# A grouped-query decode kernel: six instructions fewer on GpSimd, credits given elsewhere, and one 16-slot piece at the end of the last V tile

## The chip, the cores and the metric

One core of a Trainium2 chip. The metric is the device time of one execution in microseconds (us), as the median over runs. The profile's span (first to last instruction of the program) is about 1.85 us shorter than that time. Engines are named PE (TensorE), DVE (VectorE), ACT (ScalarE), POOL (GpSimd) and SP (SyncE). One run of the kernel before, at 670.34 us with a granted clock of 0.554 (0.80 to 0.82 in its other runs), was slow and is left out everywhere.

## The reference

Decode attention for 32 query heads in 8 groups, one query each, 65,536 keys, head width 128, bfloat16:

```python
B, Hq, Hkv, Sq, Sk, D = 1, 32, 8, 1, 65536, 128
k = jnp.repeat(k, rep, axis=1); v = jnp.repeat(v, rep, axis=1)
scores = jnp.einsum("bhqd,bhkd->bhqk", q, k) * D ** -0.5
return jnp.einsum("bhqk,bhkd->bhqd", softmax(scores), v)
```

K and V are 268 MB together and each byte is read once (the page: 268.44 MB read from HBM).

## The kernel before

K and V stream through three 8 MB buffers (`io`). A tile is half a group's K or V: 128 partitions with 256 slots of 128 values each. SP issues all loads. DVE transposes K, PE scores it, ACT takes the exponential, and PE multiplies with V. PE and DVE run loops. SP, ACT and POOL run straight through their programs. Semaphores are taken (waited for and subtracted), so a loop pass that has no load of its own for a piece finds credits there that some engine gave earlier.

The last V tile comes in pieces, so that PE can follow the landings closely:

```python
TAIL = 32
CUTS = [0, 128, 192, 224, 232, 240, 248, 252, 256]
...
pe.matmul(out=pl, lhsT=sel[:, :], rhs=vs[:, ...], start=True, stop=True).then_inc(s_pt, 1)
for t in range(SL - TAIL, SL):            # the last 32 slots: "the four-column products"
    if t in CUTS:
        pe.wait_ge(s_v[CUTS.index(t)], 16)
    if t == CUTS[-2]:
        pe.wait_ge(s_dv, d_last)          # DVE's sum of what the wide products made
        gather(D, start=False, stop=False)
    i = pe.matmul(out=fin, lhsT=et[:, 1, w0:w0 + H], rhs=io[:, t, :], ...)
i.then_inc(s_pe, 1)
```

POOL clears four buffers, makes an identity, gives initial credits, and then fills the score weights `wz` once per group (eight times 4 copies):

```python
GP.mark(gp.memset(wz[:, :, :], 0.0))
GP.mark(gp.memset(vs[:, :], 0.0))
GP.mark(gp.memset(ex[:, :, :], 0.0))
GP.mark(gp.memset(vy[:, :, :], 0.0))
n = GP.mark(gp.memset(ident[:, :], 0.0))
... identity ...
gp.sem_inc(s_vd, 2)
gp.sem_inc(s_cl, 1)
for s in (s_k[1, 64], s_k[1, 192]):
    gp.sem_inc(s, 16 * (G - 1))
gp.sem_inc(s_v[1], 16 * (2 * G - 3))
gp.sem_inc(s_v[2], 16)
...
for g in range(G):
    ...  GP.wait((s_sc, 16 * g)); gp.sem_inc(s_sd, 1); at g == 1 four more credits
    for a in range(4): gp.tensor_copy(wz ...)
```

Of the kernel before, what the change touches and what calls it, by code (L numbers as in the profile page):

```python
# [15 lines left out]
P = 128  # L16
D = 128
SL = 256
KEYS = P * SL
G = 8  # L20
# [1 line left out]
WB = 160  # L22
PS = 64
TAIL = 32
CUTS = [0, 128, 192, 224, 232, 240, 248, 252, 256]


class Queue:
# [21 lines left out]
def kernel(  # L50
# [9 lines left out]
    fp32 = mybir.dt.float32  # L60
    bf16 = mybir.dt.bfloat16
# [4 lines left out]
    def sb(name, shape, dt):  # L66
        return ctx.enter_context(nc.sbuf_tensor(name, shape, dt))
# [4 lines left out]
    def sem(name):  # L72
        return ctx.enter_context(nc.semaphore(name))
# [12 lines left out]
    nrow = sb("nrow", [1, 32, H], fp32)  # L86
    nmb = sb("nmb", [P, 1], fp32)
    rl = sb("rl", [H, 1], fp32)
    ex = sb("ex", [P, 4, 512], bf16)
    et = sb("et", [P, 2, 512], bf16)  # L90
    vs = sb("vs", [P, D + 2], fp32)
    vy = sb("vy", [P, D, 4], fp32)
    vz = vy[:, :, :].rearrange("p d y -> p (d y)").rearrange("p (y d) -> p y d", d=D)
    fall = sb("fall", [H, G - 1, D + 2], fp32)
    r7 = sb("r7", [H, G - 1], fp32)
# [9 lines left out]
    s_q, s_st = sem("s_q"), sem("s_st")  # L105
    s_v = [sem(f"s_v{i}") for i in range(len(CUTS) - 1)]
    s_dv, s_ac, s_gp = sem("s_dv"), sem("s_ac"), sem("s_gp")
# [3 lines left out]
    s_sc, s_pe, s_vb, s_vc = sem("s_sc"), sem("s_pe"), sem("s_vb"), sem("s_vc")  # L111

    s_sd, s_vd, s_pt, s_ex, s_ds = sem("s_sd"), sem("s_vd"), sem("s_pt"), sem("s_ex"), sem("s_ds")
    s_cl, s_ga = sem("s_cl"), sem("s_ga")

    def down(eng, which, s, n, wait=False):

        w = dict(sync_type="semaphore", id=s.num, ant_name=s.name)
        eng.add_instruction(mybir.InstEventSemaphore(  # L119
            name=nc.get_next_instruction_name(), engine=which, sync_info=mybir.SyncInfo(  # L120
                on_wait=[mybir.SyncWait(wait_mode="sem-ge-imm", wait_value=n, **w)] if wait else [],
                on_update=[mybir.SyncUpdate(update_mode="sem-sub-imm", update_value=n, **w)],
            ),
        ))

    sp, act, dve, gp, pe = nc.sync, nc.scalar, nc.vector, nc.gpsimd, nc.tensor
# [3 lines left out]
    GP = Queue(nc, gp, s_gp)  # L130
# [5 lines left out]
    def load(src, g, b, at, s, lo=0, hi=SL):  # L136
        sp.dma_start(  # L137
            out=io[:, at * SL + lo:at * SL + hi, :], in_=rows(src, g, b)[:, lo:hi, :]
        ).then_inc(s, 16)


    k_lo = [0, 64, 128, 192]
    s_k = {(b, lo): sem(f"s_k{b}_{lo}") for b in range(2) for lo in k_lo}

    def load_k(g, b):
        SP.wait((s_sc, 16 * g - 8 + 8 * b if g else 0))
        cuts = k_lo + [SL] if (g, b) in ((0, 0), (G - 1, 1)) else [0, 128, SL] if g == 0 else [0, SL]
        for lo, hi in zip(cuts, cuts[1:]):
            load(k, g, b, 1 + b, s_k[b, lo], lo, hi)

    def values_done(n):
        SP.wait((s_vc, n))
        if n:
            sp.sem_inc(s_vd, 1)  # L154

    def load_v(g, b):
        done = 2 * (2 * g + b)
        if (g, b) == (G - 1, 1):
            SP.wait((s_vc, done - 1))
            load(v, g, b, 0, s_v[0], CUTS[0], CUTS[1])  # L160
            values_done(done)
            down(sp, mybir.EngineType.SP, s_v[2], 16)
            for lo, hi, s in list(zip(CUTS, CUTS[1:], s_v))[1:]:
                load(v, g, b, 0, s, lo, hi)
        elif (g, b) in ((G - 2, 1), (G - 1, 0)):
            SP.wait((s_vc, done - 1))
            load(v, g, b, 0, s_v[0], 0, 128)
            values_done(done)
            load(v, g, b, 0, s_v[1], 128, SL)
        else:  # L170
            values_done(done)
            load(v, g, b, 0, s_v[0])

    load_k(0, 0)
    load_k(0, 1)
    for g in range(1, G):
        for b in range(2):
            load_k(g, b)
            load_v(g - 1, b)
# [4 lines left out]
    act.dma_start(out=q_in[:, :], in_=q[0, :, 0, :]).then_inc(s_q, 16)  # L184

    GP.mark(gp.memset(wz[:, :, :], 0.0))
    GP.mark(gp.memset(vs[:, :], 0.0))
    GP.mark(gp.memset(ex[:, :, :], 0.0))
    GP.mark(gp.memset(vy[:, :, :], 0.0))
    n = GP.mark(gp.memset(ident[:, :], 0.0))  # L190
    GP.after(n)
    p_ident = GP.mark(gp.affine_select(
# [1 line left out]
        pattern=[[-1, P]], channel_multiplier=1,  # L194
    ))

    gp.sem_inc(s_vd, 2)
    gp.sem_inc(s_cl, 1)

    for s in (s_k[1, 64], s_k[1, 192]):  # L200
        gp.sem_inc(s, 16 * (G - 1))
    gp.sem_inc(s_v[1], 16 * (2 * G - 3))

    gp.sem_inc(s_v[2], 16)
# [6 lines left out]
    n = DV.mark(dve.tensor_reduce(  # L211
        out=selq[:, :], in_=ident[:, :].rearrange("p (x r) -> p r x", r=16), axis=AX.X, op=ALU.add
    ))
# [12 lines left out]
    def d_sum(g):  # L226
        return d_qT + 4 * g + 1
# [13 lines left out]
    def take(eng, which, s, n=1):  # L241
        down(eng, which, s, n, wait=True)
# [109 lines left out]
    for t in range(SL - TAIL, SL):  # L352
# [3 lines that stand above are left out]
            pe.wait_ge(s_dv, d_last)  # L356
# [103 lines left out]
    for i in range(2):  # L460
        n = DV.mark(dve.reciprocal(out=r7[:, i::2], in_=fall[:, i::2, D + i]))
    DV.after(n)
    n = DV.mark(dve.tensor_tensor(
        out=o7, in0=fall[:, :, 0:D], in1=r7[:, :, None].to_broadcast([H, G - 1, D]),
        op=ALU.mult,
    ))
# [5 lines left out]
    n = DV.mark(dve.tensor_tensor(  # L472
        out=vz, in0=vacc, in1=sely[:, :, None].to_broadcast([P, 4, D]), op=ALU.mult
    ))
    DV.after(n)
    n = DV.mark(dve.tensor_tensor(
        out=vz[:, 0:2, :], in0=vz[:, 0:2, :], in1=vz[:, 2:4, :], op=ALU.add
    ))
    DV.after(n)
    n = DV.mark(dve.tensor_tensor(  # L480
        out=vs[:, 0:D], in0=vz[:, 0, :], in1=vz[:, 1, :], op=ALU.add
    ))
# [4 lines left out]
    n = ACTQ.mark(act.activation(out=o[:, :], in_=fin, func=ACT.Copy, scale=rl[:, :]))  # L487
# [5 lines left out]
    for g in range(G):  # L493
        if g == 0:
            GP.wait((s_dv, d_qT))
            GP.after(p_ident)
        else:
            GP.wait((s_sc, 16 * g))
            gp.sem_inc(s_sd, 1)
            if g == 1:  # L500

                for t in k_lo[1:]:
                    gp.sem_inc(s_k[0, t], 16 * (G - 1))
                gp.sem_inc(s_k[1, 128], 16 * (G - 2))
        for a in range(4):
            r = slice(32 * a, 32 * a + 32)
            c0 = 28 + 32 * a
            if a == 3 and g == 1:

                take(gp, POOL, s_et)  # L510
            if a == 3:

                GP.wait((s_dv, d_sum(g)))
            gp.tensor_copy(  # L514
                out=wz[r, :, c0:c0 + H].rearrange("p (s w) h -> p s w h", s=2),
                in_=qTb[r, :, :, g, :],
            ).then_inc(s_w, 1)
# [34 lines left out]
```

## Time and profile before

| | before |
|---|---|
| median of the first three runs | 630.37 us (629.66 to 630.48) |
| span of the profiled run | 627.7 us |
| data stream, first to last packet | 1.99 to 623.77 us |
| PE, DVE busy | 57%, 55% |

The page first: the busy share of the 16 DMA engines (in tenths) and their rate in 40 slices of the span, then the DMA queues with packets, MB and share of the engines' time.

```profile
DMA  8999999999999999999999999999999999999996
GB/s 362 441 468 401 468 401 468 401 468 401 468 401 464 405 459 409 447 422 447 422 438 430 426 443 409 459 405 464 401 468 401 468 401 468 396 437 434 434 432 274
...
q1 hardware_dynamic: 6944, 268.45, 99.2%
...
q14 instruction: 2, 0.02, 0.0%
```

The kernel is bound by its DMA stream: every slice but the first and last is 90% busy or more, nearly all of it queue q1, SP's loads. What is not about the stream itself can only matter before its start, after its end, or by taking a DMA engine's time from it. The last of these shows in the DMA view of 0 to 620 us:

```profile
q1 hardware_dynamic: 6163, 267.28, 99.9%
...
q14 instruction: 1, 0.01, 0.0%
```

The last line is one instruction packet of 8 KB (0.01 MB) in the middle of the stream. The packet records of the trace place it at 518.16 us, lasting 309 ns. The trace has 16 landing records for each load, one for each of the 16 DMA engines, and the load's semaphore is waited for at 16, so these records tell how far the slowest engine is behind the others:

```
kernel before, landings of one load on 16 engines (us): second-last, last, difference
load landing before the packet    506.86   506.90   0.04
next load                         526.25   526.54   0.29
...
last piece of the last V tile     623.85   624.11   0.26
```

One engine falls behind and does not catch up (0.26 to 0.29 us in all loads from there on, but for one of 0.22), because no engine is idle from the stream's start to 620 us (q1 alone is 99.9% of the 16 engines' time). A load counts as landed only when its slowest engine is done: PE's wide products of the tail start at 621.48, behind the last landing of their piece at 621.43; the second-last was at 621.14.

The packets of the engine that falls behind can be followed by their times, as each starts within 5 ns of the end of the one before it.

```
kernel before, packets of that engine (us): start, end, ns, bytes
515.740  518.166  2426  65,536   load
518.163  518.472   309   8,192   instructions
518.469  521.238  2769  65,536   load (all other 64 KB packets of the run: 2418 to 2524 ns)
```

The instruction packet takes 0.31 us, and the load packet behind it 0.35 us more than the usual 2.42: 0.65 us in all. The engine had been 0.32 us ahead of the slowest (whose packet ended at 518.49), so it is only 0.33 us behind now. The difference of the last two landings is thus a lower bound for what a fetch takes from its engine.

The chain of waits that ended last is the tail (start, duration, what):

```profile
609.01 12.42 DMA io<-in_v_dram
...
621.48 1.03 PE acc L254 x6
...
622.53 1.80 PE pf L359 x28
624.33 0.23 PE pf L248 x2
624.56 0.24 PE pf L359 x4
...
624.89 0.36 ACT o L487
```

A DMA landing releases PE's wide products at 621.48, then come 28 four-column products, the gather over `vs` (two matmuls), the last four products, and ACT's output.

### The profile page before, as it was taken

What the parts mean: (1) busy time and instruction counts of PE and PEld (TensorE: products, weight loads), DVE (VectorE), ACT (ScalarE), POOL (GpSimd) and SP (SyncE); (2) the same over time, 40 slices, a digit from 0 to 9 for tenths busy, and PEclk for the clock granted to TensorE, in tenths of its full rate; (3) what the DMA queues carried; (4) which work ended last, traced back from release to release, by engine and by line L of the source; (5) the groups of instructions that cost most, each with busy time, mean ns of one, the idle gap of its engine ahead of it and who ended that gap; (6) DMA issues with size and microseconds to landing.
All of it is one profiled execution on the core that took longest, in us unless ns stands there. A gap on an engine that the chain in (4) does not pass through costs nothing. (4 is left out here: it accounts for less than half of the span.)

```text
span 627.7 us, 7067 instructions
## 1 busy us (share of the span) xinstructions
PE 356.4 (57%) x2142; PEld 139.8 (22%) x2142; DVE 345.5 (55%) x154; ACT 34.4 (5%) x26; POOL 9.7 (2%) x42
## 2 busy tenths in 40 slices
PE   1865483827638275381844808458193571886346
PEld 0322131312213032130321303123031230332112
DVE  7795835649066490764807557084670946684210
ACT  0000100020000200002000020000200002000100
POOL 2000000000000000000000000000000000000000
PEclk9978595967959678596785958859587695899676
DMA  8999999999999999999999999999999999999996
GB/s 362 441 468 401 468 401 468 401 468 401 468 401 464 405 459 409 447 422 447 422 438 430 426 443 409 459 405 464 401 468 401 468 401 468 396 437 434 434 432 274
DMA packets 7003, 268.49 MB, mean 428 GB/s; under 512 B 856, under 2 KB 1112, under 8 KB 1496
## 3 DMA queue, kind: packets, MB, share of 16 engines
q1 hardware_dynamic: 6944, 268.45, 99.2%
q8 instruction: 1, 0.02, 0.0%
q14 instruction: 2, 0.02, 0.0%
q10 hardware_dynamic: 56, 0.01, 0.0%
HBM read 268.44 MB, written 0.01 MB: 428 GB/s over the span
## 5 line engine op out<-in xcount | busy, mean ns | idle before, releaser
L301 PE MATMUL acc<-io,wz 128*128 x1024 | 272.7, 420 | 184.8 <-PEq L119 157.3
L373 DVE STREAM_TRANSPOSE io<-io 128x4096 uint32<-128x4096 uint32 x64 | 279.9, 4416 | 157.2 <-DVEq L119 157.2
L301 PEld LDWEIGHTS acc<-io,wz 128*128 x1024 | 106.4, 104 | 351.2 <-issue 272.5
L254 PE MATMUL acc<-io,et 128*16 128x512 bf16 x1016 | 72.5, 416 | 19.3 <-PEq L119 19.2
L440 ACT ACTIVATE ex<-acc,nmb 128x2048 bf16<-128x2048 f32 x8 | 15.7, 1967 | 556.9 <-DVE nmb L420 556.9
L410 DVE TENSOR_REDUCE mg<-acc 128x1 f32<-128x2048 f32 x8 | 18.3, 2291 | 48.3 <-DVEq L119 48.3
L254 PEld LDWEIGHTS acc<-io,et 128*16 128x16 bf16 x1016 | 27.7, 94 | 58.4 <-issue 35.5
L248 PE MATMUL pf<-vs,sel 128*4 128x130 f32 (+1 forms) x20 | 5.7, 386 | 54.2 <-PEq L119 54.2
L376 DVE STREAM_TRANSPOSE et<-ex 128x1024 bf16<-128x1024 bf16 x17 | 20.8, 1225 | 22.6 <-SPq L154 12.8
L450 ACT ACTIVATE acc<-wz 128x2560 f32<-128x2560 bf16 (+2 forms) x8 | 16.3, 2040 | 1.0 <-ACT ex L440 0.2
L412 DVE TENSOR_REDUCE m<-pt 1x4 f32<-1x128 f32 x8 | 2.2, 279 | 22.7 <-DVEq L119 22.7
L514 POOL COPY wz<-qT 32x16 bf16<-32x16 bf16 x32 | 6.1, 189 | 512.6 <-PE acc L301 440.3
L248 PEld LDWEIGHTS pf<-vs,sel 128*4 128x4 f32 x20 | 1.2, 83 | 54.7 <-issue 54.6
L326 PE MATMUL pt<-et 128*16 128x512 bf16 x32 | 13.1, 411 | 0.0
L384 DVE TENSOR_REDUCE vs<-vy 128x128 f32<-128x512 f32 x9 | 6.1, 681 | 7.6 <-DVEq L119 7.6
L423 DVE TENSOR_TENSOR vy<-acc,sely 128x512 f32<-128x512 f32 x8 | 8.5, 1064 | 0.0
L472 DVE TENSOR_TENSOR vy<-acc,sely 128x512 f32<-128x512 f32 x1 | 0.7, 691 | 11.5 <-PE acc L254 11.5
L343 PE MATMUL pb<-ident,nrow 1*128 1x1 f32 x8 | 1.6, 194 | 7.5 <-PEq L119 7.5
L326 PEld LDWEIGHTS pt<-et 128*16 128x16 bf16 x32 | 3.1, 97 | 4.5 <-issue 1.4
L341 PE MATMUL pt<-ident,mg 128*1 128x128 f32 x8 | 2.3, 283 | 2.6 <-PEq L119 2.6
L420 DVE COPY nmb<-pb 128x1 f32<-128x1 f32 x8 | 1.3, 157 | 3.9 <-DVEq L119 3.9
L343 PEld LDWEIGHTS pb<-ident,nrow 1*128 1x128 f32 x8 | 1.1, 139 | 8.9 <-issue 8.9
(31 smaller groups left out, 22.8 us busy)
## 6 DMA issues: line engine op xcount, KB each, us to landing
io<-in_v_dram SPq DMA_DIRECT2D x5, 4096.0 KB, 16.9
io<-in_k_dram SPq DMA_DIRECT2D x8, 2048.0 KB, 27.4
io<-in_k_dram SPq DMA_DIRECT2D x2, 4096.0 KB, 34.4
io<-in_v_dram SPq DMA_DIRECT2D x1, 2048.0 KB, 10.3
io<-in_v_dram SPq DMA_DIRECT2D x1, 1024.0 KB, 12.4
io<-in_v_dram SPq DMA_DIRECT2D x3, 256.0 KB, 12.8
io<-in_v_dram SPq DMA_DIRECT2D x2, 128.0 KB, 12.8
io<-in_k_dram SPq DMA_DIRECT2D x13, 48.4
```

What stands on the lines that cost most here:

```text
L248: return pe.matmul(out=pf[0:H, 0:w], lhsT=sel[:, :], rhs=vs[:, 0:w], skip_group_check=True, **kw)
L254: return pe.matmul(out=vacc[32 * c:32 * c + 16, :, :], lhsT=et[:, ch // 2, w0:w0 + 16], rhs=io[:, PS * ch + 4 * tt:PS * ch + 4 * tt + 4, : ...
L301: i = pe.matmul(out=bass.AP(acc, r_o, [[2560, P], [1, 512]]), lhsT=bass.AP(wz, r_w + ((2 * s + e) * WB - 4 * u), [[4 * WB, P], [1, P]]), r ...
L326: pe.matmul(out=pt[0:16, :], lhsT=et[:, 0, 0:16], rhs=et[:, 0, :], start=True, stop=True)
L373: dve.transpose(out=part, in_=part).then_inc(s_kt, 2)
L376: dve.transpose(out=et[:, :, :].rearrange("p i n -> p (i n)"), in_=ex[:, 2 * b:2 * b + 2, :].rearrange("p i n -> p (i n)"),).then_inc(s_et, 1)
L384: DV.mark(dve.tensor_reduce(out=vs[:, 0:D], in_=vy[:, :, :], axis=AX.X, op=ALU.add))
L410: dve.tensor_reduce(out=mg[:, :], in_=sc, axis=AX.X, op=ALU.max).then_inc(s_mg, 1)
L423: dve.tensor_tensor(out=vy[:, :, :].rearrange("p d y -> p y d"), in0=vacc, in1=sely[:, :, None].to_broadcast([P, 4, D]), op=ALU.mult,).the ...
L440: act.activation(out=ex[:, :, :].rearrange("p b n -> p (b n)"), in_=sc, func=ACT.Exp, bias=nmb[:, :], scale=SCALE, accum_out=vs[:, D + g % ...
L450: act.activation(out=part, in_=wz[:, 0, 0:1].to_broadcast([P, part.shape[1]]), func=ACT.Copy).then_inc(s_cl, 1)
L514: gp.tensor_copy(out=wz[r, :, c0:c0 + H].rearrange("p (s w) h -> p s w h", s=2), in_=qTb[r, :, :, g, :],).then_inc(s_w, 1)
```

## The change

Its intent, as far as the diff shows it: make POOL's program shorter without making any other longer. Three clears become one; one credit comes from that clear, one from SP; the credits of four semaphores become those of two that both K tiles share. SP gets one semaphore instruction more, and the merge of two 8-slot pieces of the last V tile takes one load from it. The diff, shortened:

```diff
-CUTS = [0, 128, 192, 224, 232, 240, 248, 252, 256]
+CUTS = [0, 128, 192, 224, 240, 248, 252, 256]
-    ex = sb("ex", [P, 4, 512], bf16)
-    vs = sb("vs", [P, D + 2], fp32)
-    vy = sb("vy", [P, D, 4], fp32)
+    zs = sb("zs", [P, 1024 + 4 * D + D + 2], fp32)
+    (ex, vy, vs are views of zs)
+    for lo in k_lo[1::2]:
+        s_k[1, lo] = s_k[0, lo]
     load_k(0, 1)
+    sp.sem_inc(s_vd, 2)
-    GP.mark(gp.memset(vs[:, :], 0.0))
-    GP.mark(gp.memset(ex[:, :, :], 0.0))
-    GP.mark(gp.memset(vy[:, :, :], 0.0))
+    gp.memset(zs[:, :], 0.0).then_inc(s_cl, 1)
-    gp.sem_inc(s_vd, 2)
-    gp.sem_inc(s_cl, 1)
-    for s in (s_k[1, 64], s_k[1, 192]):
-        gp.sem_inc(s, 16 * (G - 1))
...
+                GP.wait((s_sc, 8))
+                for t in k_lo[1::2]:
+                    gp.sem_inc(s_k[0, t], 16 * (2 * G - 2))
...
-                for t in k_lo[1:]:
-                    gp.sem_inc(s_k[0, t], 16 * (G - 1))
+                gp.sem_inc(s_k[0, 128], 16 * (G - 1))
```

## The prediction

> **What bounds the kernel.** The DMA stream. The page's slice row shows the 16 DMA engines 90% busy in every slice but the first and last. The packet records show one queue moving data from 1.99 to 623.77 us without a gap: 16.8 MB an engine, 2.42 us per 64 KB, is 619.5 us. Compute is elastic: PE 57%, DVE 55%. So the change can act only on (a) the stream's start, (b) what else occupies a DMA engine, (c) packet overhead, (d) the tail after the last landings.

> **What the change does.**
> 1. Start: GpSimd fills vs, ex and vy in 0.21 + 1.81 + 0.52 us (timeline). One fp32 fill of 1,666 columns should take about 1.7 us (estimate, from 1.02 ns a column of vy). But the first K piece is taken only at 8.39 us, VectorE being ready since 7.2: worth 0.
> 2. Credits for K slots 64 and 192 of the second tile now come when PE has scored the first tile (32.9 us, when SyncE's wait for that count ended). VectorE needs the first at 37.3: worth 0.
> 3. Instruction fetches. The packet records hold an 8 KB instruction packet at 518.16 us, 309 ns long. Before it the last of 16 engines' landings trails the second-last by 0.04 us (506.90, 506.86); after it by about 0.27 us to the end (624.11, 623.85 for the last V piece). I take it for GpSimd's fetch, triggered near its instructions at 512.1 to 512.8. [...] here packets are 8 KB (one of 16). Six instructions fewer put the same place of the program at 594 to 612 us, or after 627. In the first case nothing is gained; in the second the last landings come 0.25 us sooner. I give the second 55%.
> 4. Two 2 KB packets (85 ns each) become one 4 KB packet (about 161 ns, estimate from 85 and 313 ns for 2 and 8 KB), 8 pairs an engine: stream 0.07 us shorter.
> 5. The tail. Slots 224-231 landed at 622.11, PE began their 4-column products at 622.37; slots 232-239 landed at 622.79. Merged, the products start about 622.75, and 28 of them at 0.056 us end near 624.32 instead of 624.15; the closing sum over vs (VectorE ready at 624.04, last landing 624.11) then waits for them. Cost 0.15 us if the fetch stays; if it goes, all landings are 0.25 us sooner and the end is about 0.1 us sooner than before.

> **Sum.** Fetch gone: about -0.1 us; fetch still inside: about +0.15. Both are below the spread of the three runs (0.82 us). Predicted 630.3 us, 629.5 to 631.0 in 8 of 10; faster by over 2%: 0.5%, within 2%: 99%, slower by over 2%: 0.5%.

> **What would show it.** Stream start still near 2.0 us, no idle DMA slice; second K tile's transposes back to back; no 8 KB packet before 623 (or one moved to 594-618) and the landing gap of the last piece 0.04-0.1 instead of 0.26 us; PE's wait before the 28 products about 0.35 us, none at slot 240; stream's end 0.07-0.35 us sooner; POOL's fills about 0.8 us shorter.

> **What would make it wrong.** The fetch is SyncE's (its issues at 516.2 to 518.4 fit too), whose program is one instruction longer from the seventh load on: then it stays. A fetch moved past the span could lengthen the end barriers[...]. PE's clock in the last 2 us (0.5 granted until 622.5) could differ. None of these reaches 1%.

That the 8 KB packet is a fetch of an engine's program was the assumption at that time; pad6, pad1 and pad_many test it. The sum stands at about -0.1 us with the fetch gone (0.15 for the tail, less 0.25 for the landings) and +0.15 with the fetch inside.

## The result, and the profile after

The changed kernel took 630.07 us (median of 6, 629.44 to 630.63), the kernel before 630.10 us (median of 6, 629.66 to 630.48). The ratio is 1.000, 95% interval 0.9987 to 1.0013: the same. (A ratio here is the mean time of one kernel's fast runs over the mean of the other's fast runs of the same rounds, so it is not quite the ratio of the medians.) The runs of a kernel tend to fall into two groups almost a microsecond apart, here 629.44 to 629.70 and 630.44 to 630.63 us for the changed kernel; below they are called the lower and the upper group.

The page after, the same without the rates:

```profile
DMA  8999999999999999999999999999999999999996
...
q1 hardware_dynamic: 6800, 268.45, 99.1%
...
q14 instruction: 2, 0.01, 0.0%
```

The stream is as full as before. The DMA view of 0 to 620 us:

```profile
q1 hardware_dynamic: 6169, 267.32, 99.9%
...
q14 instruction: 1, 0.00, 0.0%
```

The 8 KB packet is gone. What is left on q14 has 0.00 MB (a packet of 40 bytes at the very start). The landing records agree: nothing happens between 506 and 526 us, and the last piece lands almost half a microsecond earlier.

```
changed kernel (us): second-last, last, difference
                                  506.74   506.75   0.01
                                  526.08   526.10   0.02
last piece of the last V tile     623.62   623.62   0.01
```

The chain that ended last:

```profile
608.59 13.68 DMA io<-in_v_dram
...
622.32 1.73 PE pf L358 x28
624.04 0.22 PE pf L247 x2
624.26 0.24 PE pf L358 x4
...
624.59 0.36 ACT o L486
```

PE now waits until 622.27 for the 16-slot piece; then the same products follow. ACT's output starts at 624.59 instead of 624.89, 0.30 us sooner. Yet the span is only 0.16 us shorter (627.57 against 627.73 in the traces), and the timed runs show nothing at all. What lies between: ACT is released from its output 0.57 us sooner (626.15 against 626.72, a part of which is the output's own: 1.18 us from issue to release against 1.44), and then 0.36 us are lost again. That loss is in the end barrier, in POOL's own records (start us, duration us, instruction):

```
before    627.112 0.017 EVENT_SEMAPHORE      changed   626.538 0.017 EVENT_SEMAPHORE
          627.190 0.017 EVENT_SEMAPHORE                626.977 0.017 EVENT_SEMAPHORE
          627.271 0.064 DRAIN                          627.063 0.112 DRAIN
```

Between the same two instructions lie 0.08 us before and 0.44 us after. The second one is the 69th instruction that POOL executes; before, the 69th was a copy that POOL reached at about 512.9 us. An 8 KB packet follows it in the changed kernel, at 627.67 us, just past the span. What is left of the gain, 0.16 us, drowns in the timed runs, which scatter over about a microsecond for either kernel; the last experiment suggests why.

The output's 1.44 or 1.18 us follow a pattern, which no run tested. Every trace has an 8 KB instruction packet shortly before the output's packets (625.31 to 625.81 us in the kernel before). Where it ends 0.73 us or more ahead of them, as in six traces with the changed one among them, the release takes 1.17 to 1.18 us from the issue. Where it ends 0.48, 0.40, 0.29 or 0.23 us ahead (cuts_only, gp_only, gap_fine, before), it takes 1.29, 1.32, 1.35 and 1.44. So 0.27 of the 0.57 us seem to be the chance of where that packet falls.

The other parts of the change. POOL's clears, before and then after (timeline: start, duration, instruction):

```profile
1.52 0.21 POOL L187 MEMSET vs<- 128x130 f32 x1
...
1.67 1.81 POOL L188 MEMSET ex<- 128x2048 bf16 x1
3.41 0.52 POOL L189 MEMSET vy<- 128x512 f32 x1
...
7.59 0.59 PE L248 MATMUL pf<-vs,sel 128*4 128x130 f32 x2 [7.59 <-PEq L119]
8.50 4.45 DVE L373 STREAM_TRANSPOSE io<-io 128x4096 uint32<-128x4096 uint32 x1 [1.34 <-DVEq L119]
```

```profile
1.52 1.49 POOL L193 MEMSET zs<- 128x1666 f32 x1
...
6.66 0.59 PE L247 MATMUL pf<-zs,sel 128*4 128x130 f32 x2 [6.66 <-PEq L121]
8.36 4.45 DVE L372 STREAM_TRANSPOSE io<-io 128x4096 uint32<-128x4096 uint32 x1 [2.13 <-DVEq L121]
```

They take 1.49 us instead of 2.5, and PE's first gather starts at 6.66 us instead of 7.59. DVE's first K transpose starts at 8.36 instead of 8.50, as its first piece lands at 8.22 instead of 8.36. In the second K tile, where the moved credits are taken, DVE's first two transposes stand back to back in both traces (8.77 us for the two).

### The profile page after: what moved, and what is told of

Same layout as the page of the kernel before. It is cut to its first block, busy times and chain, and to the rows that moved or that the text cites. A ratio compares the mean times of both kernels' runs of the same rounds, so it can differ in the third digit from the quotient of the medians.

```text
span 627.6 us, 7061 instructions
## 1 busy us (share of the span) xinstructions
PE 350.0 (56%) x2142; PEld 137.9 (22%) x2142; DVE 345.5 (55%) x154; ACT 34.4 (5%) x26; POOL 8.8 (1%) x40
## 5 line engine op out<-in xcount | busy, mean ns | idle before, releaser
L300 PE MATMUL acc<-io,wz 128*128 x1024 | 268.1, 412 | 190.0 <-PEq L121 160.3
L300 PEld LDWEIGHTS acc<-io,wz 128*128 x1024 | 104.8, 102 | 353.4 <-issue 273.6
L253 PE MATMUL acc<-io,et 128*16 128x512 bf16 x1016 | 70.9, 409 | 20.4 <-PEq L121 19.3
L439 ACT ACTIVATE zs<-acc,nmb 128x2048 bf16<-128x2048 f32 x8 | 15.7, 1967 | 556.7 <-DVE nmb L419 556.7
L247 PE MATMUL pf<-zs,sel 128*4 128x130 f32 (+1 forms) x20 | 5.7, 387 | 53.3 <-PEq L121 53.3
L375 DVE STREAM_TRANSPOSE et<-zs 128x1024 bf16<-128x1024 bf16 x17 | 20.8, 1225 | 21.9 <-SPq L158 12.1
L449 ACT ACTIVATE acc<-wz 128x2560 f32<-128x2560 bf16 (+2 forms) x8 | 16.3, 2040 | 1.0 <-ACT zs L439 0.2
L383 DVE TENSOR_REDUCE zs<-zs 128x128 f32<-128x512 f32 x9 | 6.1, 681 | 7.6 <-DVEq L121 7.6
L422 DVE TENSOR_TENSOR zs<-acc,sely 128x512 f32<-128x512 f32 x8 | 8.5, 1066 | 0.0
L471 DVE TENSOR_TENSOR zs<-acc,sely 128x512 f32<-128x512 f32 x1 | 0.7, 691 | 11.6 <-PE acc L253 11.6
```

What stands on the lines that cost most here:

```text
L247: return pe.matmul(out=pf[0:H, 0:w], lhsT=sel[:, :], rhs=vs[:, 0:w], skip_group_check=True, **kw)
L253: return pe.matmul(out=vacc[32 * c:32 * c + 16, :, :], lhsT=et[:, ch // 2, w0:w0 + 16], rhs=io[:, PS * ch + 4 * tt:PS * ch + 4 * tt + 4, : ...
L300: i = pe.matmul(out=bass.AP(acc, r_o, [[2560, P], [1, 512]]), lhsT=bass.AP(wz, r_w + ((2 * s + e) * WB - 4 * u), [[4 * WB, P], [1, P]]), r ...
L375: dve.transpose(out=et[:, :, :].rearrange("p i n -> p (i n)"), in_=ex[:, 2 * b:2 * b + 2, :].rearrange("p i n -> p (i n)"),).then_inc(s_et, 1)
L383: DV.mark(dve.tensor_reduce(out=vs[:, 0:D], in_=vy[:, :, :], axis=AX.X, op=ALU.add))
L422: dve.tensor_tensor(out=vy[:, :, :].rearrange("p d y -> p y d"), in0=vacc, in1=sely[:, :, None].to_broadcast([P, 4, D]), op=ALU.mult,).the ...
```

## The experiments

### pad6: the change with POOL's old length

```diff
     gp.sem_inc(s_v[2], 16)
+    for i in range(6):
+        gp.sem_inc(s_pad, 1) if i % 2 == 0 else down(gp, POOL, s_pad, 1)
```

> The changed kernel with six idle semaphore instructions (plus one, minus one) added to GpSimd's program near its start, nothing else. Theory A (the 8 KB packet at 518 us is GpSimd's own fetch, tied to the place in its program where instruction 69 as counted on the engine stands): the packet is back between 512 and 520 us, the last of the 16 landings trails the second-last by 0.25 to 0.3 us from there to the end, the last landing moves from 623.6 to about 623.9 us, and the 0.44 us between GpSimd's two semaphore instructions of the end barrier (626.54 and 626.98 in the changed kernel, 0.08 in the kernel before) falls back to 0.08. Rival B (the fetch was SyncE's, or went away with the memsets or the credits): no instruction packet between 0 and 620 us and gap under 0.1 us. Span 627.4 to 627.9 with A, as the later landing and the shorter barrier nearly cancel.

Measured: the packet is back, at 515.66 us; the landing difference goes from 0.00 (506.82) to 0.26 (526.45) and is 0.23 at the last piece (623.97). POOL's barrier instructions are 0.08 us apart again. Span 627.5 us, ratio 1.000 (0.9986 to 1.0014). So the fetch is POOL's and goes with the length of its program; rival B falls. The clears and credits of the change are in this kernel, and so is the merged piece: against cuts_only below, which has the old clears and credits, its last landing differs by 0.04 us (623.97 and 624.01). They are worth nothing that shows.

### gp_short: six more instructions off POOL

The credits for the V pieces and those after the first tiles moved to ACT:

```diff
-    gp.sem_inc(s_v[1], 16 * (2 * G - 3)); gp.sem_inc(s_v[2], 16)
+    act.sem_inc(s_v[1], 16 * (2 * G - 3)); act.sem_inc(s_v[2], 16)
-    (POOL at g == 1: wait for s_sc 8, two credits; after s_sc 16, two more)
+    (the same waits and credits on ACT, ahead of its first exponential)
```

> The changed kernel with six more instructions taken off GpSimd (its initial credits for the V pieces and all credits after the first tiles now come from ScalarE, which has time). Theory A: instruction 69 now lies behind the program's last, so there is no instruction packet before 620 us, landings as in the changed kernel (last about 623.6, gap under 0.1), and the end barrier's two semaphore instructions of GpSimd are 0.08 us apart instead of 0.44: span about 627.2 us, 0.36 less than the changed kernel. Rival C (the 0.44 us in the barrier is chance, not a fetch): it is 0.08 or 0.4 without regard to the program's length, and span stays at 627.6. If time outside the span counts, the timed runs may gain nothing: A alone says -0.36 us, within noise of single runs (two groups 0.8 us apart).

Measured: no packet in the stream, last landing 623.55, difference 0.01, barrier instructions 0.08 us apart, span 627.09 us. Rival C falls: the gap comes and goes with the program's length. But the time outside the span rose from 1.86 us (629.36 and 627.5 for a run of before) to 2.36 us (629.46 and 627.1). The lower group of its runs, 629.46 to 629.63, is no better than before's. So the 0.36 us won inside the span are lost outside it. Most likely the stall has moved past the span's end and is still paid: the packet records reach past it and show one 8 KB packet more there than in before (628.11 and 628.13 us, against 628.75 alone). A rival stays, as ACT's program is six instructions longer in this run, and no run separates the two. Ratio 1.0008 (0.9994 to 1.0022).

### cuts_only: the merged piece alone

```diff
-CUTS = [0, 128, 192, 224, 232, 240, 248, 252, 256]    (in the kernel before)
+CUTS = [0, 128, 192, 224, 240, 248, 252, 256]
```

> The kernel before with only the two 8-slot pieces merged into one of 16. The fetch at about 518 us stays, gap 0.25 to 0.3 us. The last landing about 0.07 us earlier than before's 624.11 (against the stream's start). PE's 4-column products begin near 622.7 instead of 622.37, no longer wait at slot 240, and PE's last product ends 0.1 to 0.2 us later than before's 624.79 if the tail term of the prediction is right; if the merge is free (rival), it ends at 624.7 to 624.8. Timed: same.

Measured: the fetch stays (515.71 us), the last landing is 0.10 us earlier than before's (624.01). The chain:

```profile
609.47 13.23 DMA io<-in_v_dram
...
622.75 1.74 PE pf L359 x28
624.48 0.22 PE pf L248 x2
624.70 0.24 PE pf L359 x4
```

The products start at 622.75 instead of 622.39, and PE's last product ends at 624.93 against 624.79: 0.14 us later, as expected. So the merge costs a little while the fetch is there. Ratio 1.0004 (0.999 to 1.0019).

### gp_only: the POOL part alone

```diff
-CUTS = [0, 128, 192, 224, 240, 248, 252, 256]    (in the changed kernel)
+CUTS = [0, 128, 192, 224, 232, 240, 248, 252, 256]
```

> The changed kernel with the two 8-slot pieces kept (the GpSimd part of the change alone; SyncE's program one instruction longer than in either kernel). No instruction packet between 0 and 620 us, gap under 0.1 us, last landing about 623.7. PE's last product near 624.4 us, within 0.1 us of the changed kernel's 624.48, as there the landing bounds it and here PE's own 28 products. If SyncE's length has a boundary of its own near its end, an 8 KB packet appears between 610 and 623 us and one engine lags 0.3 us again; I expect none. Timed: same.

Measured: no packet in the stream though SP's program is one instruction longer, difference 0.01 to 0.03, last landing 623.66.

```profile
620.94 1.02 PE acc L253 x5
...
621.99 1.89 PE pf L358 x28
623.88 0.22 PE pf L247 x2
624.10 0.24 PE pf L358 x4
```

The products start at 621.85 to 621.99, wait once for their second piece, and end 0.16 us before the changed kernel's (last end 624.32 against 624.48). The barrier gap is 0.44 us as in the changed kernel. Ratio 1.0001 (0.9987 to 1.0015). So in this pair of traces the POOL part alone gains 0.47 us at PE's last product (624.32 from 624.79), of which the merge gives back 0.16; the barrier's 0.36 come on top in both. These sizes are of single traces and no larger than the spread between traces. Without the fetch in the stream, and with PE at full clock from about 622.5 us on, PE's last product ends at 624.32, 624.45 and 624.47 us with the two pieces (gp_only, shadow_fine, gap_fine) and at 624.41, 624.48 and 624.65 with the one (gp_short, the changed kernel, shadow): the merge costs 0.1 us in the mean, and the two sets overlap. The fetch is clearer: the last landing is at 623.55 to 623.82 us in the seven traces without it in the stream, and at 623.97 to 624.15 in the four with one.

### pad1: one instruction more

```diff
     gp.sem_inc(s_v[2], 16)
+    gp.sem_inc(s_pad, 1)                  (in the changed kernel)
```

> The changed kernel with one idle instruction more in GpSimd's program. If the boundary is exactly its 69th instruction, GpSimd now reaches it at 611.1 us, when it starts to wait in the end barrier: an 8 KB packet appears between 611.5 and 618 us, and the last of 16 landings trails by 0.25 to 0.3 us from that piece on only (none before). If the boundary lies elsewhere: no packet, or one at 575 to 600.

Measured: the packet is at 615.50 us, and only the loads landing after it show the lag (0.01 at 613.62, 0.53 at 619.06, 0.49 at the end, 624.15). The boundary is the 69th instruction exactly. The lag is more than the packet's 309 ns, and more than I expected: the 16 KB load packet behind the fetch took 961 ns where the others take about 0.61 us, so the engine lost 0.66 us again. This was a single run with a single profile, and that profile turned out to be of the upper group (630.85 us): see after_again.

### pad_many: twenty-one fetches more

```diff
             ).then_inc(s_w, 1)
+        if g < G - 1:
+            for i in range(384): (idle semaphore instruction, in turn plus and minus one)
```

> The changed kernel with 384 idle semaphore instructions after each of GpSimd's first seven groups (2,688 in all, about 30 us a group, in time it spends waiting). At 128 instructions a packet: 21 packets of 8 KB in the span. If all load the same DMA engine and each takes it 0.31 us from the stream, the last landing trails the second-last by about 6 us and the timed runs are 5.5 to 7 us (0.9 to 1.1%) slower than before. If the packets are spread over the engines, the gap and the loss are under 1 us.

Measured: 21 packets of 8 KB in the stream, the first at 13.69, 24.04 and 34.42 us. That is one for 128 of the 2,688 instructions, which the expectation had only assumed. POOL's own records show the other half of it: every 128 instructions one step takes 0.37 to 0.44 us instead of 0.08. This stall is not a wait for the packet: the first one ends at 10.17 us and the packet starts at 13.69. (With the DMA engines free, the packet starts about 1.13 us after the last instruction before the stall: 627.67 after 626.54 in the changed kernel.) The landing difference grows in steps, to 1.70 us after 3 fetches (load landed at 44.04), 3.65 after 6 (104.05), 5.62 after 9 (183.44) and 7.59 after 12 (262.79). So the fetches fall on one DMA engine, and each costs it 0.63 us (7.59 over 12), twice the packet's 0.31. The packet records say where the other half goes: at 11 of the first 12 fetches the load packet behind it took about 0.35 us longer than its like (2.77 instead of 2.42 us for 64 KB), at the other 0.27. From 293 us on other load packets are longer too. Time 646.9 us, ratio 1.0259 (1.0243 to 1.0276): with enough of them the timed runs see the mechanism clearly. My expectation of 5.5 to 7 us was wrong, as it took the packet's duration for the cost. At 0.63 us, 21 fetches are 13.2 us; the last landing is 16.3 us later than the changed kernel's. In the second half the other engines are late too (the second-last landing also slips, and the difference falls back to 3.5 us). Loads are issued when a buffer is free, and a buffer is free when its slowest engine has delivered, so a large lag should run the others dry in the end; the mean busy share of the DMA engines does fall to 0.96 between 500 and 600 us (1.00 in the changed kernel). PE also had half its clock from 594 us to 641.8. That a fetch shows as 0.53 us in pad1 but only 0.25 to 0.36 in before, pad6 and cuts_only is no contradiction: in all four the load packet behind it is 0.34 to 0.35 us longer, and the difference of the last two landings shows only what is left after that engine's lead. Why the packet behind a fetch is longer, and how the other 3 us divide, stays open.

### shadow and shadow_fine: the fetch after PE's last product

```diff
     gp.sem_inc(s_w, 4)
+    GP.wait((s_pe, 1))
+    for i in range(4): (idle semaphore instruction)
```

`shadow` is this in the changed kernel, `shadow_fine` the same with the two 8-slot pieces.

> The changed kernel with a wait for PE's last product and four idle semaphore instructions at the end of GpSimd's program, so that its 69th instruction is reached at about 624.5 us: after the data stream, and 2 us before the end barrier. If the 0.44 us in the barrier of the changed kernel is GpSimd's stall at its 69th instruction, and the 0.5 us by which the shortest GpSimd program (the run gp_short) lost outside the span what it had won inside is the same stall in the code after the span, then here: no instruction packet before 620 us, GpSimd's extra instructions show one gap of about 0.35 us, barrier instructions 0.08 us apart, span about 627.15 us, and the time outside the span stays at 1.85 us: about 629.0 us in the lower of the two groups of runs, against 629.2 to 629.6 of before. Rival: the shortest program's 0.5 us outside the span has another cause (ScalarE's longer program, say), or the stall falls wherever it is later; then 629.4.

> The same with the two 8-slot pieces kept as before the change (GpSimd part alone plus the shadowed fetch). As the run with the 16-slot piece, PE's last product about 0.1 us sooner (624.32 against 624.48 in the two runs without the shadow): span about 627.05. Timed 628.9 to 629.1 in the lower group; no difference to the other that timed runs could show.

Measured: no packet in the stream, POOL's stall is where I put it (0.44 us between 624.85 and 625.29), the barrier gap is 0.08. But the span is 628.3 us, not 627.15, and the runs' median 630.13. The time went into the output: ACT issued it at 625.14 and was released at 627.25, 2.1 us later; in the changed kernel it was 624.97 and 626.15, 1.2 us. The fetch's packet (625.98, 418 ns) lies among the output's own packets (625.90 on), and the last of the four starts at 626.40, when the fetch's ends, instead of 0.06 us after the first. In shadow_fine it is the same: 625.78 for the fetch, 626.19 for the last output packet, span 628.0. So the shadow was not one: in both runs a packet of 0.4 us ahead of a 256-byte write came with a release 0.7 to 0.9 us later, more than its own length. Ratios 1.0008 (0.9994 to 1.0021) and 0.9997 (0.9983 to 1.0011). Both expectations of the time were wrong.

### gap_fine: the fetch between the last landing and the output

```diff
     gp.sem_inc(s_w, 4)
+    GP.wait((s_dv, d_last - 1))
+    for i in range(4): (idle semaphore instruction)
-CUTS = [0, 128, 192, 224, 240, 248, 252, 256]    (in the changed kernel)
+CUTS = [0, 128, 192, 224, 232, 240, 248, 252, 256]
```

> The GpSimd part of the change with the two 8-slot pieces kept, and the fetch placed once more: GpSimd waits for VectorE's second-last sum (about 623.2 us) and runs four idle semaphore instructions, so that it reaches its 69th instruction at about 623.4, between the last landing (623.66) and the output's packets (625.6). Theory: its packet lies at 624.0 to 625.2, GpSimd stalls 0.4 us where nobody waits, the output's packets are not delayed (issue to ScalarE's release 1.3 us, as in the kernel before, against 2.1 in the run shadow), barrier instructions 0.08 us apart, span about 627.2 us when PE has its full clock in the tail, time outside the span 1.85 us: about 629.0 us in the lower group of runs, 0.3 below the lower group of the changed kernel. Rival: any fetch after the stream still costs its 0.4 us somewhere; then 629.4.

Measured: POOL stalls from 623.49 to 623.93 while nobody waits for it, its packet and the one that every trace has there lie at 624.64 and 624.91 (the first is POOL's by its distance, 1.15 us after POOL's last instruction before the stall, 1.13 in the changed kernel), the output's packets start at 625.71 and stay together, ACT is released 1.35 us after it issues the output, and the barrier instructions are 0.08 us apart. No instruction packet lies in the stream before 620 us. The chain's end:

```profile
622.11 1.83 PE pf L359 x28
623.95 0.30 PE pf L248 x2
624.24 0.24 PE pf L359 x4
...
624.57 0.36 ACT o L487
```

The five runs took 628.84 to 629.10 us, median 628.96; the nine runs of before took 629.28 to 630.37, median 629.51. Ratio 0.9989, 95% interval 0.9976 to 1.0003. Every run is below every run of before, also of the other calls (lowest 629.16), and below every run of the changed kernel in the same call (629.42 to 630.31, after_again). The size (about 0.3 us from the lowest group of before) is what was expected; the interval itself still holds 1, because before's runs scatter.

### after_again: the changed kernel once more

> The changed kernel once more, on the same chip as the other of this call. No instruction packet before 620 us, no jump of the landing gap, two GpSimd barrier instructions 0.4 us apart, time outside the span 1.85 us; same as before within 0.15%. Its runs fall into two groups 0.8 to 1.1 us apart; if the group is set by PE's granted clock in the last 3 us, a profile of the upper group shows the 32 four-column products at 0.107 us each instead of 0.056.

Measured: 629.64 us, ratio 1.000 (0.9986 to 1.0014), barrier gap 0.44 us again, last landing 623.74. This time the profiled run was one of the upper group (630.31 us, span 628.4). The four-column products in the first profile of the changed kernel, and in this one (the source-line view: instruction, count, duration in ns least, median, most, first and last start):

```profile
L358 PE MATMUL pf<-io,et x32: 218/219/219, 622.3 to 624.3; 128*4 128x128 bf16 x32
```

```profile
L358 PE MATMUL pf<-io,et x32: 219/309/311, 622.3 to 625.1; 128*4 128x128 bf16 x32
```

And the windows of the tail (busy time by engine, then the granted PE clock, DMA share and GB/s), first of the first profile, then of this one:

```profile
622.00:623.00 1.00, 0.68 (x13) 0.69 (x14) 0.93 (x3) 0.00 (x0) 0.00 (x0) 1.00 0.99 333
623.00:624.00 1.00, 1.00 (x21) 0.98 (x19) 0.22 (x2) 0.00 (x0) 0.00 (x0) 1.00 0.09 25
624.00:625.00 1.00, 0.48 (x7) 0.27 (x4) 0.00 (x0) 0.36 (x1) 0.00 (x0) 1.00 0.03 8
```

```profile
622.00:623.00 1.00, 0.76 (x11) 0.74 (x9) 0.91 (x2) 0.00 (x0) 0.00 (x0) 0.50 0.98 330
623.00:624.00 1.00, 1.00 (x12) 1.00 (x10) 0.57 (x3) 0.00 (x0) 0.00 (x0) 0.50 0.11 24
624.00:625.00 1.00, 1.00 (x17) 0.95 (x15) 0.00 (x0) 0.00 (x0) 0.00 (x0) 0.90 0.03 8
```

The stream ends alike in both (last landings 623.62 and 623.74), and the 28 products start within 0.05 us of each other (622.32, 622.26), but at a clock of 0.5 they take 2.63 us instead of 1.73, and everything behind them is 0.9 us later. The profile of pad1, the only other one whose run lay in an upper group, shows the same (28 products in 2.64 us). In the clock records of the kernel before and of the changed kernel, PE's clock is granted at 1.0 or 0.5, in stretches that are whole multiples of 3.41 us (but for the last, which the end cuts off). In the tail of the kernel before, the clock goes from 0.5 to 1.0 at 622.80 us; three of the last steps from product to product before it are 0.106 or 0.107 us, and those after it mostly 0.055 to 0.057. What makes the clock change was not shown. That the upper group of timed runs as a whole is this was not shown for each run, since timed runs leave no clock of their last 3 us; two profiles of two fit.

## Why the prediction was right

- The bound (DMA stream, compute elastic): right. The stream starts at 1.98 us and is full in both.
- Clears and credits worth 0 (steps 1 and 2): right. PE's first gather was 0.93 us earlier and nothing downstream moved with it; pad6 against cuts_only confirms it.
- The instruction fetch (step 3): right, and now shown. It is POOL's (pad6, pad1), tied to the 69th instruction that the trace lists, and it left the stream for a place after 627 us (627.67), as the likelier of the two cases said. Its price was read too low: 0.25 us of later landings, where the engine lost 0.65. POOL's packets are of 8,192 bytes, one every 128 instructions (21 for 2,688 in pad_many); the one instruction packet of 16,384 bytes in the trace of the kernel before came on another queue (q8, at 623.05 us). The prediction gave "gone from the stream" only 55%, by guessing where six instructions would put it; the right answer followed from the count and the 69th place, which it did not work out.
- The packet term (step 4): a 4 KB packet took 159 ns against the estimated 161; the last landing came 0.10 us sooner in cuts_only, 0.07 predicted.
- The tail term (step 5): 0.15 us predicted, 0.14 measured with the fetch (cuts_only) and 0.16 without (gp_only); over all traces it is nearer 0.1, within their spread.
- The sum, "about -0.1 us": the span fell by 0.16. That agreement is luck: here two mis-sized terms nearly cancelled. PE's last product came 0.30 us sooner, not 0.1 (0.14 to 0.38 in the three such traces), the output's release came another 0.27 sooner, and the end barrier gave back 0.36, which the prediction had only as a possibility ("A fetch moved past the span could lengthen the end barriers"). POOL's stall at the boundary was not in the sum at all.
- The size of the noise: the prediction named PE's clock in the last 2 us as a risk (0.5 until 622.5 by its windows; the clock record has the change at 622.80). In the two profiles that show it, it moves the end by 0.9 us, more than anything that the change does.

## What to carry to other kernels

When a DMA stream is full from start to end, what else passes through a DMA engine can be added to the end, even 8 KB of instructions (0.65 us of one engine here, 0.25 to 0.53 at the last landing of a load), less the lead which that engine has over the slowest; count each engine's instructions and see in the packet records when its next block is fetched. Moving such a fetch is not removing it: POOL also stalled for some 0.4 us (0.37 to 0.44), and in a barrier (0.36 us, the changed kernel), among the output's packets (0.7 to 0.9, shadow and shadow_fine) or, as it seems, past the last instruction (0.5, gp_short) that was paid too, so put it where neither the data nor another engine waits (gap_fine: about 0.3 us won, though its interval holds 1). And before explaining half a microsecond between runs, look at the clock that PE had in the tail (0.9 us between the two profiles of the changed kernel).
